# Loads cut by partitions: attention chunks in four transfers of 32, weight blocks in two of 64

## The chip, the cores and the metric

The kernel runs on one core of a Trainium2 chip. The time is that of one execution on the device in microseconds (us); a kernel's time is the median of its runs.

## The reference

The computation has two parts. The first is a linear attention (retention) with a decaying state per batch and head; the second is an MLP whose values are gated by a short convolution over time.

```python
gamma = 1.0 - 2.0 ** (-5.0 - np.arange(H))          # B, H, S, D = 4, 8, 768, 64
for t in range(S):
    state = gamma * state + einsum('bhd,bhe->bhde', k[:, :, t], v[:, :, t])
    y[:, :, t] = scale * einsum('bhd,bhde->bhe', q[:, :, t], state)
x = y.transpose(0, 2, 1, 3).reshape(B, S, H * D)     # 4 x 768 x 512
gate_pre = sum over k < 5 of conv_w[k] * xp[:, k:k + S, :]   # xp: x behind 4 rows of zeros
out = (sigmoid(gate_pre) * (x @ w_val)) @ w_out      # both weights 512 x 512
```

All inputs are float32; the two weight matrices and the convolution's weights reach the kernel as 64-bit words and are converted to float32 on the chip.

## The kernel before, in words

**Attention.** The sequence of each of the 4 batches is cut into 6 chunks of 128 tokens. Chunk number g (0 to 23) runs over the batches first: chunks 0 to 3 are the first 128 tokens of the four batches. `load(g)` (L163 to L168) brings a chunk's q, k by dimension, v and k by token into one tile `att` of 128 partitions with 8 KB each, 1,024 KB in all; chunk 0 comes in two halves of 4 KB rows. There are five such tiles (`LB`), so chunk g + 5 is loaded into the tile of chunk g when that is done with. Then GpSimd multiplies v by a decay (`decay`, L183), TensorE makes the scores (L193), VectorE masks them (`u`, L203), TensorE multiplies by v (L231), adds to the state `z_ps` (L215), ScalarE copies the state (`snap`, L226), TensorE reads it with q (L231), and VectorE moves the result into `x` (`evac`, L276). ScalarE and GpSimd split x into two parts for TensorE, `xh` (L287) and the remainder `xl` (L293).

**Weights.** `load_w(n)` (L300 to L306) brings one of eight blocks, 128 partitions with 4 KB each, 512 KB in all, into one of four `wst` tiles; blocks 0 to 3 are `w_val`, 4 to 7 `w_out`. Six steps, mostly on VectorE (L326, L332, L338, L342, the flush L355) with one on ScalarE (L347) and the sum on GpSimd (L351), make float32 values of it, then ScalarE and GpSimd split them (`wvh` or `woh` at L366, `wvl` or `wol` at L370).

**MLP.** It works in 6 units of 128 tokens of all batches, 4 tiles each. A tile has the convolution (`acc`, L381 on ScalarE and L383 on VectorE), the sigmoid (`gate`, L390, two buffers), the value product (L400, 12 matrix products), the gating (L414), the split of the gated values (`gvh` L417, `gvl` L421) and, a unit later, the output product (L431), a copy (L441) and the store (L445). The sigmoid of tile m reuses the gate buffer of tile m - 2, which GpSimd's L421 has read last. There are two x buffers.

**Order.** Each step is entered with a due time, an engine, a cost and the names that it reads and writes. `plan` makes one order of all steps from these, once, and each engine then works through its own steps strictly in that order. All transfers are issued by SyncE, in order too. A step that loads is one step in the plan, whatever `load` and `load_w` issue for it, so the plan doesn't know how a load is cut. The first loads stand in the plan as chunk 0, small tables, chunk 1, block 0, chunk 2, blocks 1 and 2, chunk 3, block 3, chunks 4 to 8, blocks 4 to 7, chunk 9, and from then on chunks and stores. At the start TensorE runs 13 matrix products without use (L451).

Of the kernel before, what the change touches and what calls it, by code (L numbers as in the profile page):

```python
# [10 lines left out]
I32 = mybir.dt.int32  # L11
# [4 lines left out]

P = 128
HALF = 64
NPAIR = 4
TAPS = 5  # L20
WARM = 13
# [3 lines left out]
TINY = 2.0 ** -15 * (1.0 + 1.0 / 8.0)  # L25
LO, HI = slice(0, HALF), slice(HALF, P)

# [51 lines left out]
def tile_retention_gated_mlp(  # L79
# [31 lines left out]
    nc = tc.nc  # L111
# [23 lines left out]
    pos_sb = const.tile([2, P + 512], F32, name="pos_sb")  # L135
    cw_sb = const.tile([P, NPAIR, TAPS], F32, name="cw_sb")
    base = const.tile([P, NPAIR, P], F32, name="base")
    wvh = const.tile([P, NPAIR, DM], F32R, name="wvh")
    wvl = const.tile([P, NPAIR, DM], F32R, name="wvl")
    woh = const.tile([P, NPAIR, DM], F32R, name="woh")  # L140
    wol = const.tile([P, NPAIR, DM], F32R, name="wol")

    z_ps = ps_s.tile([P, 2, B, 2, HALF], F32, name="z_ps")
    sy0 = ps_y.tile([P, 2, 512], F32, name="sy")
# [16 lines left out]
    tiles, us, snaps, xs, xh, xl, decs, pos_ps = {}, {}, {}, {}, {}, {}, {0: base}, []  # L161

    def load(g, part=slice(0, 4)):  # L163
        b, c = chunks[g]
        i = b * NCH + c
        if part.start == 0:
            tiles[g] = loads.tile([P, 4, 2, 2, P], F32, name="att")
        nc.sync.dma_start(out=tiles[g][:, part], in_=att[i, :, part])  # L168

    def get(dst, src):  # L170
        nc.sync.dma_start(out=dst, in_=src)
# [5 lines left out]
    def sy_of(g):  # L177
        return sy1 if g < EARLY and g % 2 else sy0

    def decay(g):  # L180
        b, c = chunks[g]
        v = tiles[g][:, 2].rearrange("p x j (s e) -> p (x j s) e", s=2)
        nc.gpsimd.tensor_tensor(  # L183
            v, v, vd_sb[:, c, :].unsqueeze(2).broadcast_to([P, 8, HALF]), op=ALU.mult
        )

    def scores(g):
        sy = sy_of(g)
        q, kT = halves(g, 0), halves(g, 1)
        for j in range(2):  # L190
            for s in range(2):
                for x, rows, cols in ((0, LO, LO), (1, HI, LO), (1, LO, HI), (0, HI, HI)):
                    nc.tensor.matmul(  # L193
                        sy[cols, x, (2 * j + s) * HALF:(2 * j + s + 1) * HALF],
                        lhsT=kT[rows, x, j, s, :],
# [4 lines left out]
    def mask(g):  # L200
        sy = sy_of(g)
        us[g] = mlp.tile([P, 2, 4, HALF], F32, name="u")
        nc.vector.tensor_tensor(  # L203
            us[g],
            sy[:, :, 0:256].rearrange("p x (a t) -> p x a t", t=HALF),
            tri_sb.unsqueeze(1).unsqueeze(1).broadcast_to([P, 2, 4, HALF]),
# [92 lines left out]

    def load_w(n):  # L300
        st = stage.tile([P, 512, 2], I32, name="wst", bufs=4)
        nc.sync.dma_start(
            out=st,
            in_=w64[n // 4, n % 4].bitcast(I32).rearrange("p (n two) -> p n two", two=2),
        )
        raws[n] = st  # L306

    cvt = {}
# [158 lines left out]
    def load_at(due, g):  # L467
        a = [("att", g % LB, "qk"), ("att", g % LB, "vk")]
        if g == 0:
            at(due, "DMA", 1.4, [], a[0:1], load, g, slice(0, 2))  # L470
            at(due, "DMA", 0.2, [], ["small"], get, small_sb, small)
            at(due, "DMA", 1.4, [], a[1:2], load, g, slice(2, 4))
            at(due, "DMA", 0.1, [], ["pos"], get, pos_sb, pos)
            at(due, "DMA", 0.1, [], ["cwraw"], get, cw_raw,
               conv_w.bitcast(I32).rearrange("p (n two) -> p n two", two=2))
        else:
            at(due, "DMA", 2.6, [], a, load, g)
# [63 lines left out]
    def load_w_at(t, n):  # L541
        at(t, "DMA", 1.3, [], [("wst", n % 4)], load_w, n)
# [60 lines left out]
    for p in range(4 * (NU - 1)):  # L603
        n, m = 1 + p // 4, p % 4
# [98 lines left out]
```

## Time and profile before

| | |
|---|---|
| Time, median of 3 runs | 237.65 us (237.08 to 238.66) |
| Profiled execution | 236.69 us, span 233.9 us |
| TensorE matmul busy | 209.4 us (90% of the span) |
| VectorE, GpSimd, ScalarE busy | 142.3, 105.9, 105.3 us |
| Read from HBM, written | 29.46 MB, 6.29 MB |
| Chunk, median from issue to landing | 5.4 us |
| Weight block, median from issue to landing | 8.7 us |

The page has the busy shares of the engines over 40 slices of the span, the traffic of the DMA engines, the chain of work that ended last, and groups of instructions. The trace behind it gives each engine's instructions in time, with the idle time before them and what ended it. Engine names in it are PE (TensorE's matrix products), PEld (its weight loads), DVE (VectorE), ACT (ScalarE), POOL (GpSimd) and SP (SyncE); a q behind a name is that engine's sequencer. TensorE's busy time counts pipelined products, so a busy TensorE isn't one at its peak.

### The profile page before, as it was taken

The page shows a single profiled execution, that of the slowest core. Times are in us where ns is not written, and L with a number is a line of the kernel's source. Part 1 is how long each engine was busy: PE and PEld are TensorE (multiplying, and loading weights), DVE is VectorE, ACT ScalarE, POOL GpSimd, SP SyncE. Part 2 cuts the span into 40 slices and gives each one's busy share as a digit, 9 for nine tenths or more (in the row PEclk, how much of TensorE's full clock was granted, in tenths as well). Part 3 has the DMA queues.
Part 4 walks back from the last instruction along what each step waited for, and adds up shares of the span by engine and source line. Part 5 has one row for each costly group of instructions (what it writes and reads, how often), then busy time and mean ns, then how long its engine had stood idle before and what let it go on. Part 6 is the DMA issues. An engine that isn't in the chain of part 4 may idle for free.

```text
span 233.9 us, 7910 instructions
## 1 busy us (share of the span) xinstructions
PE 209.4 (90%) x3547; PEld 163.2 (70%) x3547; DVE 142.3 (61%) x214; ACT 105.3 (45%) x210; POOL 105.9 (45%) x93
## 2 busy tenths in 40 slices
PE   8574779975955999999999999999999999999994
PEld 2363667754643877777777877877877778888884
DVE  0288879999699882699325895318991269811100
ACT  2333384554627362754346744237532456322222
POOL 0358986479929464543464254434413442222200
PEclk9778559997997999999999999999999999999999
DMA  5999968546540254653354346321011101111122
GB/s 159 387 418 415 402 251 331 181 134 230 186 179 1 84 205 168 227 224 129 115 216 182 95 177 228 132 101 48 0 48 48 47 1 61 63 58 45 45 90 90
DMA packets 8677, 36.24 MB, mean 155 GB/s; under 512 B 1090, under 2 KB 1474, under 8 KB 5700
## 3 DMA queue, kind: packets, MB, share of 16 engines
q1 hardware_dynamic: 8644, 35.75, 41.0%
q8 instruction: 27, 0.44, 0.8%
q14 instruction: 6, 0.05, 0.1%
HBM read 29.46 MB, written 6.29 MB: 153 GB/s over the span
## 4 chain that ended last, share of the span: by engine, by line
PE 79%; DVE 8%; DMA 5%; issue 4%; POOL 2%; SPq 1%; ACT 0%; ACTq 0%; DVEq 0%; POOLq 0%
PE mm L400 31%; PE mm L431 29%; PE sy L231 10%; PE z_ps L215 5%; DMA att<-in_att_dram 5%; PE sy L193 4%; DVE acc L383 1%; DVE u L203 1%; POOL rest L351 1%; DVE acc L338 1%; DVE rest L355 1%; DVE top L332 1%; DVE rest L342 1%; DVE x L276 1%; DVE acc L326 1%
## 5 line engine op out<-in xcount | busy, mean ns | idle before, releaser
L383 DVE SCALAR_TENSOR_TENSOR acc<-x,cw_sb,acc 128x512 f32<-128x512 f32 x96 | 71.0, 753 | 7.3 <-ACT acc L381 5.1
L421 POOL TENSOR_TENSOR gvl<-gate,gvh 128x512 fp32r<-128x512 f32 x24 | 31.0, 1292 | 43.1 <-ACT gvh L417 43.1
L293 POOL TENSOR_TENSOR xl<-x,xh 128x512 fp32r<-128x512 f32 x24 | 30.9, 1286 | 39.6 <-ACT xh L287 39.6
L431 PE MATMUL mm<-woh,gvh 128*128 128x512 f32 (+1 forms) x100 | 39.0, 390 | 4.9 <-ACT woh L366 4.9
L431 PE MATMUL mm<-wol,gvh 128*128 128x512 f32 (+1 forms) x100 | 39.0, 390 | 0.0
L431 PE MATMUL mm<-woh,gvl 128*128 128x512 f32 (+1 forms) x100 | 38.9, 389 | 0.0
L183 POOL TENSOR_TENSOR att<-att,small_sb 128x512 f32<-128x512 f32 x24 | 25.0, 1044 | 25.7 <-DMA att<-in_att_dram 24.4
L276 DVE TENSOR_TENSOR x<-sy,dec 128x512 f32<-128x512 f32 x20 | 13.7, 687 | 36.8 <-PE sy L193 29.3
L226 ACT COPY snap<-z_ps 128x256 f32<-128x256 f32 x44 | 16.1, 371 | 32.5 <-PE z_ps L215 32.5
L400 PE MATMUL mm<-xl,wvh 128*128 128x512 f32 x96 | 30.2, 411 | 0.0
L400 PE MATMUL mm<-xh,wvl 128*128 128x512 f32 x96 | 28.5, 413 | 0.0
L400 PE MATMUL mm<-xh,wvh 128*128 128x512 f32 x96 | 28.4, 420 | 0.1
L441 ACT COPY o_sb<-mm 128x512 f32<-128x512 f32 (+1 forms) x25 | 14.3, 571 | 27.3 <-PE mm L431 27.0
L414 DVE TENSOR_TENSOR gate<-mm,gate 128x512 f32<-128x512 f32 x24 | 16.5, 685 | 16.2 <-PE mm L400 16.1
L231 PEld LDWEIGHTS sy<-u,att 64*64 64x64 f32 x768 | 15.7, 153 | 13.6 <-issue 4.4
L431 PEld LDWEIGHTS mm<-woh,gvh 128*128 128x128 f32 x100 | 18.9, 189 | 8.9 <-ACT woh L366 5.3
L287 ACT CAST xh<-x 128x512 fp32r<-128x512 f32 x24 | 14.9, 620 | 21.9 <-DVE x L276 21.8
L215 PE MATMUL z_ps<-att 64*64 64x64 f32 x704 | 22.0, 242 | 2.6 <-issue 1.5
L231 PE MATMUL sy<-u,att 64*64 64x64 f32 x768 | 18.9, 244 | 6.1 <-DVE x L276 3.1
L215 PEld LDWEIGHTS z_ps<-att 64*64 64x64 f32 x704 | 17.0, 151 | 8.7 <-issue 5.0
L417 ACT CAST gvh<-gate 128x512 fp32r<-128x512 f32 x24 | 14.8, 618 | 18.2 <-DVE gate L414 18.2
L193 PE MATMUL sy<-att 64*64 64x64 f32 x768 | 17.9, 232 | 5.5 <-issue 2.8
(42 smaller groups left out, 264.7 us busy)
## 6 DMA issues: line engine op xcount, KB each, us to landing
att<-in_att_dram SPq DMA_DIRECT2D x23, 1024.0 KB, 5.4
out_dram<-o_sb SPq DMA_DIRECT2D x23, 256.0 KB, 2.0
wst<-in_w_dram SPq DMA_DIRECT2D x8, 512.0 KB, 8.7
att<-in_att_dram SPq DMA_DIRECT2D x2, 512.0 KB, 5.4
out_dram<-o_sb SPq DMA_DIRECT2D x2, 128.0 KB, 1.7
small_sb<-in_small_dram SPq DMA_DIRECT2D x1, 68.0 KB, 4.1
cw_raw<-in_conv_w_dram SPq DMA_DIRECT2D x1, 20.0 KB, 5.9
pos_sb<-in_pos_dram SPq DMA_DIRECT2D x1, 5.0 KB
```

Of the source, the lines that this page charges most:

```text
L183: nc.gpsimd.tensor_tensor(v, v, vd_sb[:, c, :].unsqueeze(2).broadcast_to([P, 8, HALF]), op=ALU.mult)
L193: nc.tensor.matmul(sy[cols, x, (2 * j + s) * HALF:(2 * j + s + 1) * HALF], lhsT=kT[rows, x, j, s, :], rhs=q[rows, x, j, s, :], start=True, ...
L215: nc.tensor.matmul(z_ps[cols, x, b, j], lhsT=k[rows, x, j, s, :], rhs=v[rows, x, j, s, :], start=g == 0 and s == 0 and j == 0, stop=True, ...
L226: nc.scalar.copy(sn, z_ps[:, :, b])
L231: nc.tensor.matmul(sy_of(g)[cols, h, off:off + HALF], lhsT=lhsT, rhs=rhs, start=start, stop=True, skip_group_check=True,)
L276: nc.vector.tensor_tensor(xs[c][:, :, b, HALO:].rearrange("p (h j) t -> p h j t", h=2), sy_of(g)[:, :, 256:512].rearrange("p h (j t) -> p ...
L293: nc.gpsimd.tensor_tensor(xl[c][:, :, b], xs[c][:, :, b, HALO:], xh[c][:, :, b].bitcast(F32), op=ALU.subtract)
L383: nc.vector.scalar_tensor_tensor(acc, x[:, :, k:k + P], cw_sb[:, m, k:k + 1], acc, op0=ALU.mult, op1=ALU.add,)
L400: nc.tensor.matmul(vps[n, m], lhsT=w[:, m, ct * P:(ct + 1) * P], rhs=xx[n][:, ct].rearrange("p b t -> p (b t)"), start=(i == 0), stop=(i = ...
L414: nc.vector.tensor_tensor(gv, vps.pop((n, m)), gv, op=ALU.mult)
L421: nc.gpsimd.tensor_tensor(gvl[:, m, :], gate.pop((n, m)), gvh[:, m, :].bitcast(F32), op=ALU.subtract)
L431: nc.tensor.matmul(ops[n, b, cs.start][:, 0:cs.stop - cs.start], lhsT=gg[:, ct, b * P:(b + 1) * P], rhs=w[:, ct, cs], start=(i == 0), stop ...
```

## The change

Each load of a chunk is issued as four transfers of 32 partitions (256 KB each; for the two halves of chunk 0, 128 KB each), each load of a weight block as two transfers of 64 partitions (256 KB each). Rows, bytes, tiles, buffers and the plan's table of steps are the same; all transfers go through SyncE's queue as before. In the changed kernel the lines behind the edits have numbers higher by one or two: the chunks' transfers are issued at L170, the blocks' at L306, the decay is L185.

```diff
+ROWS = 32
...
     def load(g, part=slice(0, 4)):
...
-        nc.sync.dma_start(out=tiles[g][:, part], in_=att[i, :, part])
+        for p in range(0, P, ROWS):
+            nc.sync.dma_start(out=tiles[g][p:p + ROWS, part], in_=att[i, p:p + ROWS, part])
...
     def load_w(n):
         st = stage.tile([P, 512, 2], I32, name="wst", bufs=4)
-        nc.sync.dma_start(
-            out=st,
-            in_=w64[n // 4, n % 4].bitcast(I32).rearrange("p (n two) -> p n two", two=2),
-        )
+        src = w64[n // 4, n % 4].bitcast(I32).rearrange("p (n two) -> p n two", two=2)
+        for p in range(0, P, 2 * ROWS):
+            nc.sync.dma_start(out=st[p:p + 2 * ROWS], in_=src[p:p + 2 * ROWS])
         raws[n] = st
```

## The prediction

> **What bounds the kernel now.** I read the page first: the busy shares over time, then what the DMA engines moved, then the chain that ended last.
>
> ```profile
> PE   8574779975955999999999999999999999999994
> DVE  0288879999699882699325895318991269811100
> POOL 0358986479929464543464254434413442222200
> DMA  5999968546540254653354346321011101111122
> GB/s 159 387 418 415 402 251 331 181 134 230 186 179 1 84 205 168 227 224 129 115 216 182 95 177 228 132 101 48 0 48 48 47 1 61 63 58 45 45 90 90
> PE 79%; DVE 8%; DMA 5%; issue 4%; POOL 2%; SPq 1%; ACT 0%; ACTq 0%; DVEq 0%; POOLq 0%
> ```
>
> Each slice is 5.85 us. From slice 13 (76 us) TensorE is full to the end, so work that reaches that phase later ends the kernel later by as much. Before it no engine is full throughout; VectorE comes nearest. The loads fill the DMA engines in slices 1 to 4, near 400 GB/s, and leave room in most slices after that. So if the change touches the loads, it acts in the first 75 us.
>
> The chain in order of time shows how the loads set that phase, and the waits show who stands there.
>
> ```profile
> 3.81 10.75 DMA att<-in_att_dram
> 14.62 1.04 POOL att L183
> 15.71 1.29 POOL rest L351
> 17.03 0.69 DVE rest L355
> POOL att L183 <- DMA att<-in_att_dram: 24.4, 15, 7.8
> ```
>
> The third chunk is issued at 3.81 and lands at 14.56; GpSimd's decay of it is released by the landing, and the weights' sum (L351) and VectorE's flush (L355) follow. GpSimd waits for chunks 15 times, 24.4 us in all. It runs in a written order: a late chunk holds up everything behind that chunk's decay, also work that doesn't need the chunk. That is where I expect a slower load to bite.
>
> **The change part by part.** No byte, matrix product or elementwise instruction is added, removed or moved; what changes is the shape of the loads and the waits on them.
>
> *Issues and waits.* SyncE issues 25 chunk transfers and 8 weight transfers now, 100 and 16 afterwards.
>
> ```profile
> att<-in_att_dram SPq DMA_DIRECT2D x23, 1024.0 KB, 5.4
> wst<-in_w_dram SPq DMA_DIRECT2D x8, 512.0 KB, 8.7
> L168 SPq DMA_DIRECT2D att<-in_att_dram x25: 327/328/752, 0.7 to 148.5; - x25
> L193 PEldq EVENT_SEMAPHORE  x5: 51/51/51, 10.8 to 59.4; - x5
> L183 POOLq EVENT_SEMAPHORE  x20: 17/17/43, 8.2 to 154.3; - x20
> ```
>
> An issue takes 0.33 us at the median, so four take 1.3 us where one took 0.33. A 256 KB piece at the 421 GB/s that are quoted below flows in 0.62 us, longer than its issue: issuing is hidden under the flow. The order also shows that every transfer waits for the one eight before it; eight are now 2 MB in flight, 5 us of flow at 421 GB/s, against the 2.9 us that a chunk takes beyond its own flow (median 5.4 us to landing, 2.5 of them flow). So the queue stays filled, and I cost this at nothing. Each reader of a chunk waits for four landings instead of one. Scores gain two separate waits of 51 ns per chunk: at most 24 x 2 x 0.051 = 2.4 us if TensorE always stands for them; at least nothing, where it still has matrix work queued. GpSimd's 17 ns waits, about three more per chunk, are 1.2 us over the whole run on an engine at 45%. I take 0.5 us for all waits in the case where nothing else happens; in the forecast they lie inside longer stalls and count nothing.
>
> *The rate of the loads* is the term that decides. No row shows a transfer onto part of the partitions, apart from 5 KB of positions. These rows are the nearest:
>
> ```profile
> 2.00:4.00 2.00, 2.00 (x6) 0.76 (x5) 0.00 (x0) 0.22 (x2) 0.00 (x0) 1.00 0.86 229
> 4.00:6.00 2.00, 1.72 (x6) 0.50 (x4) 0.00 (x0) 0.00 (x0) 0.00 (x0) 1.00 0.86 245
> 10.00:20.00 10.00, 5.98 (x237) 5.44 (x241) 7.81 (x13) 3.71 (x9) 5.88 (x5) 0.75 1.02 421
> ```
>
> The last two columns are the DMA engines' busy share and GB/s. With whole chunks and blocks in the queue the engines move 421 GB/s. In the first 4 us, with chunk 0's halves and small tables one behind the other, they are busy 86% and move only 229 to 245: busy engines can run at little more than half of the rate. From above, the bound is the 421. From below: if each of the 128 partitions accepts no more than it does today, a piece on 32 is held to a quarter, 105 GB/s. If all DMA engines work on a piece, as they do on a chunk, they write to the same 32 partitions together and afterwards to the next 32, so I expect crowding, though not down to a quarter: nothing shows that partitions, rather than engines, are at their limit now. I take the row of short transfers, 229.
>
> [...]
>
> *From the rate to the end.* On SyncE's queue, in the place where chunk 8, the second four weight blocks and chunk 9 are loaded, before:
>
> ```order
> L168 DMA att<-in_att_dram 128x2048 [waits DMAHW0_49,DMAHW2_49,PE_49,Pool_49]
> L302 DMA wst<-in_w_dram 128x1024 [waits DMAHW1_49,Activation_49]
> L302 DMA wst<-in_w_dram 128x1024 [waits Activation_49]
> L302 DMA wst<-in_w_dram 128x1024 [waits DMAHW3_49,Activation_49]
> L302 DMA wst<-in_w_dram 128x1024 [waits DMAHW4_49,Activation_49]
> L168 DMA att<-in_att_dram 128x2048 [waits DMAHW5_49,PE_49,Pool_49]
> ```
>
> And changed, from the second of those weight blocks to chunk 9:
>
> ```order
> L306 DMA wst<-in_w_dram 64x1024 [waits DMAHW5_49,Activation_49]
> L306 DMA wst<-in_w_dram 64x1024 [waits DMAHW6_49]
> L306 DMA wst<-in_w_dram 64x1024 [waits DMAHW7_49,Activation_49]
> L306 DMA wst<-in_w_dram 64x1024 [waits DMAHW0_49]
> L306 DMA wst<-in_w_dram 64x1024 [waits DMAHW1_49,Activation_49]
> L306 DMA wst<-in_w_dram 64x1024 [waits DMAHW2_49]
> L170 DMA att<-in_att_dram 32x2048 [waits DMAHW3_49,PE_49,Pool_49]
> ```
>
> DMAHW0 to 7 are the eight landing semaphores, used in turn; the order of transfers is the same, and chunk 9 still comes behind chunks 1 to 8 and all eight weight blocks. On GpSimd the order is the same too; here are the decays of chunks 7, 8 and 9 (the last row) with the first remainder of gated values (gvl) between them, before and changed:
>
> ```order
> L370 TENSOR_TENSOR wvl<-rest,wvh 128x512 [waits Activation_49] x2
> L183 TENSOR_TENSOR att<-att,small_sb 128x512 [waits DMAHW7_49,PE_49]
> L183 TENSOR_TENSOR att<-att,small_sb 128x512 [waits DMAHW0_49,PE_49]
> L421 TENSOR_TENSOR gvl<-gate,gvh 128x512 [waits Activation_49]
> L183 TENSOR_TENSOR att<-att,small_sb 128x512 [waits DMAHW5_49,PE_49]
> ```
>
> ```order
> L371 TENSOR_TENSOR wvl<-rest,wvh 128x512 [waits Activation_49] x2
> L185 TENSOR_TENSOR att<-att,small_sb 128x512 [waits DMAHW5_49,DMAHW4_49,DMAHW6_49,DMAHW3_49,PE_49]
> L185 TENSOR_TENSOR att<-att,small_sb 128x512 [waits DMAHW2_49,DMAHW1_49,DMAHW7_49,DMAHW0_49,PE_49]
> L422 TENSOR_TENSOR gvl<-gate,gvh 128x512 [waits Activation_49]
> L185 TENSOR_TENSOR att<-att,small_sb 128x512 [waits DMAHW5_49,DMAHW4_49,DMAHW6_49,DMAHW3_49,PE_49]
> ```
>
> Each decay waits for four landings now, and nothing else has moved. The issue of chunk 9, the decays of chunks 0 and 9, and what stands behind the latter on GpSimd, ScalarE, VectorE and TensorE (start, duration, in brackets the idle time before it):
>
> ```profile
> 40.67 8.84 SPq L168 DMA_DIRECT2D att<-in_att_dram  x2
> 8.27 1.04 POOL L183 TENSOR_TENSOR att<-att,small_sb 128x512 f32<-128x512 f32 x1 [7.83 <-DMA att<-in_att_dram]
> 45.66 1.04 POOL L183 TENSOR_TENSOR att<-att,small_sb 128x512 f32<-128x512 f32 x1 [1.99 <-DMA att<-in_att_dram]
> 46.66 1.29 POOL L421 TENSOR_TENSOR gvl<-gate,gvh 128x512 fp32r<-128x512 f32 x1
> 54.12 1.28 POOL L351 TENSOR_TENSOR rest<-rest,top 128x512 f32<-128x512 f32 x1
> 48.95 0.60 ACT L390 ACTIVATE gate<-acc 128x512 f32<-128x512 f32 x1
> 50.83 0.68 DVE L414 TENSOR_TENSOR gate<-mm,gate 128x512 f32<-128x512 f32 x1
> 55.40 0.68 DVE L276 TENSOR_TENSOR x<-sy,dec 128x512 f32<-128x512 f32 x1
> 59.87 0.69 DVE L276 TENSOR_TENSOR x<-sy,dec 128x512 f32<-128x512 f32 x1 [1.87 <-PE sy L231]
> 72.64 0.49 PE L431 MATMUL mm<-woh,gvh 128*128 128x512 f32 x1 [4.85 <-ACT woh L366]
> ```
>
> Chunk 0 is decayed at 8.27 in either kernel, since its stretch already runs at 229 to 245. Behind it, up to chunk 9, come nine chunks of 1.049 MB and eight blocks of 0.524 MB. At 229 GB/s a chunk takes 4.58 us and a block 2.29, together 41.2 + 18.3 = 59.5, so chunk 9 is decayed at 67.8 and not at 45.66: 22.1 later. Its buffer doesn't set this: it is free for the issue at 40.67 now, and would have to come free over 20 us later. Behind the decay L421 ends at 68.8 + 1.3 = 70.1. The fourth sigmoid reuses the gate buffer that L421 has read (two buffers), 70.1 to 70.7, then VectorE's L414 starts at 70.7, where it stood at 50.83: 19.9 later. The other 2.2 us were slack between L421, sigmoid and L414. From there VectorE works almost without a gap to 72 us, through the conversions of the output weights; its one larger gap (1.87 us at 59.87) is a round trip to TensorE that itself began with L276 at 55.40, so it moves along, and the sum L351 at 54.12 moves by 20.9 on GpSimd. TensorE's stand of 4.85 us ends with weights from that same work. Nothing takes the delay back before TensorE is full.
>
> Later loads are hidden even at that rate:
>
> ```profile
> 99.52 0.33 SPq L168 DMA_DIRECT2D att<-in_att_dram  x1
> 104.96 1.04 POOL L183 TENSOR_TENSOR att<-att,small_sb 128x512 f32<-128x512 f32 x1 [0.59 <-DMA att<-in_att_dram]
> 110.01 1.29 POOL L421 TENSOR_TENSOR gvl<-gate,gvh 128x512 fp32r<-128x512 f32 x1 [4.00 <-ACT gvh L417]
> ```
>
> A chunk issued at 99.52 would be decayed at 108.1 in place of 104.96 (1.0 us of later issue, 4.58 for 2.49 us of flow), to 109.1, and GpSimd's next work starts at 110.01.
>
> The sum: 19.9 us. On the profiled execution (236.69 us, span 233.9) that makes 256.6; that run lies 0.4% under the median of 237.65 (237.08 to 238.66), and on the median it makes **257.5 us**.
>
> **The rivals.** The rate at which the delay begins follows from the same rows: chunk 9 may be 2.2 us late, so 13.6 MB must flow in 39.6 us, 344 GB/s.
>
> [...]
>
> (2) Partial overlap. With eight pieces queued, engines drift apart, and the rate is midway between 229 and 421, 325 GB/s: chunk 3.23, block 1.61, chunk 9 at 50.2, 4.6 late, less 2.2: +2.4, 240.0 us.
>
> (3) The pieces cost nothing: the rate stays above 344, only waits are left, 238.2 us. For it: a piece still runs on all engines, and the bytes per row are the same, 8 KB. Against: nothing quoted shows partial transfers at speed.
>
> (4) Faster: the 229 to 245 GB/s at the start come from large transfers behind each other, and pieces lift them to 421. Chunk 0 with its tables (1.14 MB) then takes 2.7 us and not 4.9; the chain from the third chunk starts 2.2 us earlier, 235.4 us. It decides only if the rate afterwards stays above 344 too; the same engines then run at 421 with large transfers, which speaks against it.
>
> **How the numbers follow.** Forecast 0.46, half rate 0.25, partial overlap 0.12, nothing 0.14, faster 0.03. The range 240 to 266 us holds the forecast and the first two rivals, 0.83; its top is a rate of about 200 GB/s. The quarter rate is left out. A measurement here can tell about 1% (2.4 us) from no change: faster 0.03, same 0.14, slower 0.83.
>
> **What would show it.** Right: GB/s near 230 in slices 2 to 11 in place of 400 and less, at the same high DMA share; the decay of chunk 9 near 68 us with a long wait for its transfer; total waits of L185 for chunks well over 24.4 us; TensorE full from about 96 us; the stretch from there to the end as long as before. Wrong: GB/s above 344 in slices 2 to 4, or chunk 9 decayed before 48 us. If chunk 9 is as late as said but TensorE is full much earlier than 96 us, my account of VectorE's order is the step that failed. If the last phase grows, the waits on TensorE weigh more than I say.

## The result and the profile after

The change makes the kernel slower: 260.39 us median (259.44 to 262.22, 4 runs) against 237.37 (236.88 to 238.66, 4 runs), ratio 1.097 with a 95% interval of 1.0894 to 1.1046. The forecast was 257.5 us (240 to 266), so slower by somewhat more than said. The profiled execution took 262.22 us, with a span of 260.3; it is the slowest of the four, and set against the one before (span 233.9) it shows +26.4 us where the medians differ by 23.0. Some runs of the kernels below took over 1.5% longer than the fastest of the same kernel; they are left out of the ratios, of the kernel with two transfers of 64 neighbours only one run (257.45 us) and no ratio remains, and the profiles of that kernel, of every fourth partition and of the alternating halves are of such runs.

First the page of the changed kernel: busy shares, DMA share and traffic over 40 slices of 6.5 us, and the shares of the chain that ended last.

```profile
PE   7573551999327929999999999999999999999995
DMA  7999999999937760786755875658001111111132
GB/s 171 219 220 230 220 209 218 219 215 243 220 71 165 174 151 3 168 227 152 190 147 137 204 165 141 170 141 204 22 21 43 43 43 40 43 40 40 40 118 86
PE 64%; DMA 25%; DVE 3%; SPq 2%; issue 2%; POOL 1%; ACT 1%; POOLq 0%; ACTq 0%; DVEq 0%
```

Slices 1 to 10 (6.5 to 71 us) are a plateau at 209 to 243 GB/s with the DMA engines busy 90% or more (digit 9); before, the loads ran near 400 and were done with their bulk in slice 6. DMA has gone from 5% of the chain to 25%. The stretches of time say the same (window, its length, busy time and count of PE, PEld, DVE, ACT and POOL, then granted TensorE clock, DMA share, GB/s):

```profile
10.00:20.00 10.00, 5.90 (x186) 5.28 (x178) 4.75 (x7) 3.32 (x9) 1.04 (x1) 0.61 1.02 214
30.00:40.00 10.00, 5.37 (x151) 4.72 (x152) 5.06 (x8) 2.13 (x4) 5.42 (x5) 0.50 1.05 222
60.00:70.00 10.00, 6.81 (x190) 4.97 (x188) 5.37 (x8) 2.23 (x5) 0.00 (x0) 0.95 1.05 234
```

A DMA share of 1.02 stands beside 214 GB/s here, and stood beside 421 before: the share tells that the engines hold packets, not how fast bytes move. In 60 to 70 us GpSimd does nothing at all. The chain in order of time shows why:

```profile
12.76 10.71 DMA wst<-in_w_dram
...
61.77 9.49 DMA att<-in_att_dram
71.42 1.04 POOL att L185
72.46 1.23 POOL gvl L422
```

Six transfers follow each other without a gap from 12.76 to 71.26, each 9 to 11 us from issue to landing, since eight transfers are in the queue at a time; the last is chunk 9's, and its decay is next. GpSimd's waits for chunks, and the instructions that the prediction followed (start, duration, idle time before):

```profile
POOL att L185 <- DMA att<-in_att_dram: 68.6, 20, 11.6
```

```profile
71.42 1.04 POOL L185 TENSOR_TENSOR att<-att,small_sb 128x512 f32<-128x512 f32 x1 [11.60 <-DMA att<-in_att_dram]
72.42 1.26 POOL L422 TENSOR_TENSOR gvl<-gate,gvh 128x512 fp32r<-128x512 f32 x1
74.34 0.69 DVE L415 TENSOR_TENSOR gate<-mm,gate 128x512 f32<-128x512 f32 x1 [7.35 <-ACT gate L391]
97.24 0.79 PE L432 MATMUL mm<-woh,gvh 128*128 128x512 f32 x1 [4.75 <-ACT woh L367]
```

Chunk 9's decay moved from 45.66 to 71.42 (+25.8), the gating from 50.83 to 74.34 (+23.5), the first output product with `woh` from 72.64 to 97.24 (+24.6). From there to the end of the span it takes 163.1 us, against 161.3 before (+1.8). 24.6 and 1.8 are the 26.4. The chain that ended last goes on from the sigmoid (73.72) through ScalarE and not through the gating: ScalarE stood 8.59 us for L422, the copy of the state stands behind that sigmoid in its order, and TensorE stands 8.21 us for the copy, up to 76.18.

### The profile page after: what moved, and what is told of

The parts are those of the page before. It is cut to its first block, busy times and chain, and to the rows that moved or that the text cites. A ratio compares the mean times of both kernels' runs of the same rounds, so it can differ in the third digit from the quotient of the medians.

```text
span 260.3 us, 8078 instructions
## 1 busy us (share of the span) xinstructions
PE 218.5 (84%) x3547; PEld 170.0 (65%) x3547; DVE 142.8 (55%) x214; ACT 105.3 (40%) x210; POOL 105.9 (41%) x93
## 3 DMA queue, kind: packets, MB, share of 16 engines
q1 hardware_dynamic: 9972, 35.76, 57.8%
## 4 chain that ended last, share of the span: by engine, by line
PE 64%; DMA 25%; DVE 3%; SPq 2%; issue 2%; POOL 1%; ACT 1%; POOLq 0%; ACTq 0%; DVEq 0%
PE mm L432 26%; PE mm L401 23%; DMA att<-in_att_dram 13%; DMA wst<-in_w_dram 11%; PE sy L233 8%; PE z_ps L217 4%; PE sy L195 3%; SPq L170 2%; DVE acc L384 1%; DVE acc L327 1%; DVE x L278 1%; DVE rest L356 1%; POOL rest L352 0%; POOL gvl L422 0%; SPq L173 0%
## 5 line engine op out<-in xcount | busy, mean ns | idle before, releaser
L185 POOL TENSOR_TENSOR att<-att,small_sb 128x512 f32<-128x512 f32 x24 | 25.0, 1044 | 76.6 <-DMA att<-in_att_dram 68.6
L422 POOL TENSOR_TENSOR gvl<-gate,gvh 128x512 fp32r<-128x512 f32 x24 | 31.0, 1293 | 34.8 <-ACT gvh L418 34.8
L432 PE MATMUL mm<-woh,gvh 128*128 128x512 f32 (+1 forms) x100 | 39.6, 396 | 4.7 <-ACT woh L367 4.7
L432 PE MATMUL mm<-wol,gvh 128*128 128x512 f32 (+1 forms) x100 | 39.6, 396 | 0.0
L217 PE MATMUL z_ps<-att 64*64 64x64 f32 x704 | 23.4, 250 | 13.5 <-ACT snap L228 8.7
L217 PEld LDWEIGHTS z_ps<-att 64*64 64x64 f32 x704 | 18.4, 159 | 19.6 <-ACT snap L228 10.2
L195 PE MATMUL sy<-att 64*64 64x64 f32 x768 | 21.5, 247 | 9.6 <-DMA att<-in_att_dram 6.8
L401 PE MATMUL mm<-xh,wvl 128*128 128x512 f32 x96 | 29.3, 423 | 0.0
L195 PEld LDWEIGHTS sy<-att 64*64 64x64 f32 x768 | 18.2, 157 | 13.1 <-issue 11.8
L233 PEld LDWEIGHTS sy<-u,att 64*64 64x64 f32 x768 | 16.5, 159 | 15.3 <-issue 4.0
L233 PE MATMUL sy<-u,att 64*64 64x64 f32 x768 | 19.8, 251 | 7.7 <-DVE u L205 2.9
L289 ACT CAST xh<-x 128x512 fp32r<-128x512 f32 x24 | 14.9, 619 | 19.9 <-DVE x L278 19.9
```

The costliest lines, as they stand in the source:

```text
L185: nc.gpsimd.tensor_tensor(v, v, vd_sb[:, c, :].unsqueeze(2).broadcast_to([P, 8, HALF]), op=ALU.mult)
L195: nc.tensor.matmul(sy[cols, x, (2 * j + s) * HALF:(2 * j + s + 1) * HALF], lhsT=kT[rows, x, j, s, :], rhs=q[rows, x, j, s, :], start=True, ...
L217: nc.tensor.matmul(z_ps[cols, x, b, j], lhsT=k[rows, x, j, s, :], rhs=v[rows, x, j, s, :], start=g == 0 and s == 0 and j == 0, stop=True, ...
L233: nc.tensor.matmul(sy_of(g)[cols, h, off:off + HALF], lhsT=lhsT, rhs=rhs, start=start, stop=True, skip_group_check=True,)
L401: nc.tensor.matmul(vps[n, m], lhsT=w[:, m, ct * P:(ct + 1) * P], rhs=xx[n][:, ct].rearrange("p b t -> p (b t)"), start=(i == 0), stop=(i = ...
L422: nc.gpsimd.tensor_tensor(gvl[:, m, :], gate.pop((n, m)), gvh[:, m, :].bitcast(F32), op=ALU.subtract)
```

## The experiments

**The theories.** *Reach*: what sets the rate is which of the 128 partitions a transfer touches; onto 32 or 64 neighbours it flows at about half, whatever its size (214 to 234 GB/s in the stretches above, 421 with whole loads). It is a theory: the trace gives rates and packet times, and not what holds a packet up. The "ways" and "paths" of the expectations below are my picture for it, and no row shows them. *Count and size*: more and smaller transfers in the queue are slower whatever they touch, because fewer bytes are in flight or each piece has a fixed cost. *Waits*: the readers' additional waits cost the time. Beside these stands the question whether the written order, chunk 9's decay ahead of L422, turns late bytes into late work.

### Cut along the row instead of by partitions

```diff
-        nc.sync.dma_start(out=tiles[g][:, part], in_=att[i, :, part])
+        for x in range(part.start, part.stop):
+            nc.sync.dma_start(out=tiles[g][:, x], in_=att[i, :, x])
...
+        for h in (slice(0, 256), slice(256, 512)):
+            nc.sync.dma_start(out=st[:, h], in_=src[:, h])
```

> Four transfers per chunk and two per block as in the change, 256 KB each, but cut along the row: each goes to all 128 partitions, with 2 KB rows. Two theories of the slow loads. Reach: a transfer onto a part of the partitions can be written at half the rate only, whatever its size; here every transfer spans all partitions, so the loads run at 380 to 420 GB/s between 10 and 30 us, chunk 9 is decayed before 48 us, and the time is 236 to 239 us. Count: it is the number of transfers, their 256 KB or the 2 MB in flight that slow the loads; then they stay at 210 to 230 GB/s and the time is 257 to 262 us. The finer pieces also let the decay of a chunk wait for its v alone, which can only help.

Measured 238.19 us (235.27 to 239.25) against 237.5, ratio 1.0003 (0.9955 to 1.0052). The stretches:

```profile
10.00:20.00 10.00, 6.13 (x224) 5.49 (x224) 7.70 (x13) 3.13 (x8) 5.67 (x5) 0.77 1.04 384
20.00:30.00 10.00, 6.52 (x224) 5.60 (x224) 8.69 (x15) 4.40 (x9) 8.19 (x9) 0.74 1.04 367
```

Nearly as many transfers as in the change, each of the same 256 KB, and the rate stays at 367 to 384 GB/s: a little under the 380 to 420 expected, above the 344 that the prediction had as its threshold. Chunk 9 is decayed at 45.58. Count and size fall as the cause. The waits are tested less fully here: a chunk lands in four pieces, but its decay waits for one to four of them, where in the change it waits for all four.

### Chunks alone, in 32 and in 64 neighbours

```diff
+        for p in range(0, P, ROWS):
+            nc.sync.dma_start(out=tiles[g][p:p + ROWS, part], in_=att[i, p:p + ROWS, part])
```

> Only the chunks are cut in four by 32 partitions, the weight blocks stay whole. With 4.87 us for a cut chunk (its landings in the changed kernel lie that far apart) and 1.25 us for a whole block at 421 GB/s, chunk 9 is decayed at 7.8 + 43.8 + 10.0 = 61.6 us, VectorE's fourth gating follows 2.9 us later at 64.5, where it stood at 50.8 before: 13.7 us later, with 1 to 2 us from later waits 251 to 253 us. If a chunk and a block don't simply add up along the queue, the time lies elsewhere: near 260 if the chunks alone set it.

The second kernel has `p` in steps of 64. Weight blocks are whole in both.

> Chunks cut in two by 64 partitions, weight blocks whole. If what counts is how many of the write ways a transfer reaches, and 64 neighbouring partitions reach no more than 32 do, the time equals that of the kernel with chunks cut by 32 and whole blocks, 251 to 253 us, with loads near 215 GB/s while chunks alone flow. If crowding goes with the number of partitions, 64 are crowded half as much: a chunk takes about 3.7 us, chunk 9 is decayed near 51 us, and the time is 239 to 242 us. By count, half as many transfers of twice the size also give the middle.

Measured 258.63 us (256.73 to 262.23), ratio 1.0885 (1.0795 to 1.0975), and 264.29 us (257.45 to 265.93); 237.5 us before. The stretch in which only chunks are loaded, 32 first, then 64:

```profile
30.00:40.00 10.00, 4.86 (x134) 4.02 (x127) 5.75 (x9) 2.13 (x4) 4.96 (x5) 0.50 1.03 216
40.00:50.00 10.00, 7.96 (x88) 6.31 (x88) 5.18 (x8) 5.58 (x13) 8.12 (x7) 0.64 1.03 220
```

```profile
30.00:40.00 10.00, 5.49 (x154) 4.93 (x155) 5.38 (x9) 2.13 (x4) 5.76 (x5) 0.50 1.02 216
40.00:50.00 10.00, 5.81 (x79) 4.87 (x79) 5.30 (x8) 5.59 (x13) 7.83 (x7) 0.57 1.02 221
```

Twice as many partitions, and twice the bytes, in each transfer buy nothing: 216 and 221 against 216 and 220. That fits the reach theory if 64 neighbours are held as far down as 32, as they are in these rows. Both times are longer than the 251 to 253 expected, though, in all eight runs; the sum that I had made for chunks alone is wrong (below).

### Every fourth and every second partition

```diff
-        for p in range(0, P, ROWS):
-            nc.sync.dma_start(out=tiles[g][p:p + ROWS, part], in_=att[i, p:p + ROWS, part])
+        for p in range(4):
+            nc.sync.dma_start(out=tiles[g][p::4, part], in_=att[i, p::4, part])
```

> Chunks cut in four transfers of 32 partitions again, but each takes every fourth partition of all 128; weight blocks whole. If crowding is by neighbouring partitions (reach), each transfer now spreads over the whole memory and the rate comes back for the most part, 330 to 421 GB/s: 237 to 241 us. If it is the number of partitions in one transfer, or their count and size, nothing changes against chunks cut by 32 neighbours: 251 to 253 us.

The second kernel has `range(2)` and `p::2`.

> Chunks in two transfers of 64 partitions, every second one (0, 2, 4, ... and 1, 3, 5, ...), weight blocks whole: same count and size as the kernel with two transfers of 64 neighbouring partitions (264.3 us, chunk 9 decayed at 68.0). If it counts which partitions a transfer reaches: above 340 GB/s from 10 to 40 us, chunk 9 decayed at 45 to 53, 237 to 241 us. If it counts how many partitions or how many bytes it has: 257 to 265 us, chunk 9 at 65 to 68.

Measured 241.09 us (239.29 to 244.16) against 237.5, ratio 1.0147 (1.0068 to 1.0226), and 237.25 us (235.37 to 238.57) against 237.43, ratio 1.0005 (0.996 to 1.0049). The stretches, fourth first, then second:

```profile
10.00:20.00 10.00, 5.86 (x205) 5.18 (x205) 4.90 (x9) 3.31 (x8) 2.35 (x3) 0.61 0.94 340
20.00:30.00 10.00, 6.35 (x236) 5.75 (x239) 8.99 (x15) 4.01 (x9) 9.26 (x8) 0.73 1.03 417
```

```profile
10.00:20.00 10.00, 5.90 (x224) 5.33 (x224) 6.79 (x11) 2.59 (x6) 5.39 (x5) 0.72 1.01 408
20.00:30.00 10.00, 5.79 (x207) 5.24 (x208) 8.35 (x14) 3.63 (x7) 7.94 (x8) 0.62 1.01 398
```

This is the cleanest pair: the same count, the same 64 partitions and 512 KB in each transfer as in the slow kernel above, other partitions, and 398 to 408 GB/s instead of 216. Which partitions a transfer touches decides here. One thing goes along with it: a transfer that leaves out partitions also leaves out the source's rows, and no run parts the two. The length of the source alone is not it, though: a whole block is 512 KB in one piece of the source, and its 4 KB packets take 160 ns (before, median from 16 to 30 us); 64 neighbours of a chunk are 512 KB in one piece as well, and their 8 KB packets take 619, twice as long per byte.

With every fourth partition the decays wait for up to four landings, as in the change, so such waits cost no more than this kernel loses. Its loss of 1.5% fits another source, the issue. Two rows of SyncE's issues (form, duration in ns as least, median and most, first and last start), of every fourth and of 32 neighbours:

```profile
L170 SPq DMA_DIRECT2D att<-in_att_dram x100: 468/592/1537, 0.7 to 159.2; - x100
```

```profile
L170 SPq DMA_DIRECT2D att<-in_att_dram x100: 310/413/1949, 0.7 to 169.6; - x100
```

(The second row is of the kernel that follows.) An issue of a strided piece takes 0.59 us at the median, and a 256 KB piece flows in 0.62 us at 421 GB/s. With the halves of chunk 0, 128 KB each, issuing is the slower of the two: this kernel moves 184 GB/s at a DMA share of 0.62 from 4 to 6 us, its chunk 1 is issued from 7.23 to 9.61 us where that was done at 2.86 before, and its decay of chunk 9 comes at 52.33.

In the stretches shown, the six kernels with cut chunks up to here fall into two groups: 214 to 234 GB/s where the pieces are of neighbouring partitions, 340 to 417 where each piece reaches over all 128.

### The order of the pieces

```diff
-        for p in range(0, P, ROWS):
+        for p in (0, 64, 32, 96):
```

> Chunks in four transfers of 32 neighbouring partitions, issued in the order 0, 64, 32, 96 instead of 0, 32, 64, 96; weight blocks whole. Same count and size as the kernel with chunks alone cut (258.6 us, chunk 9 decayed at 66.05). If pieces in the queue overlap and each meets another part of the partitions' paths, consecutive pieces on different halves run side by side: the rate climbs toward 330 to 420 GB/s, chunk 9 is decayed at 46 to 54, 238 to 247 us. If every DMA engine works through its queue one packet after another, the order of the pieces changes nothing: 257 to 260 us, chunk 9 at 65 to 68.

Blocks are whole, as in the kernel with chunks alone cut. Measured 253.22 us (251.04 to 254.94) against 237.43, ratio 1.0625 (1.0549 to 1.0702): between the two expectations.

```profile
30.00:40.00 10.00, 4.87 (x135) 4.20 (x137) 5.75 (x9) 2.13 (x4) 4.76 (x5) 0.50 1.02 244
40.00:50.00 10.00, 8.49 (x89) 6.94 (x88) 7.15 (x11) 6.87 (x15) 10.00 (x9) 0.60 1.03 243
```

244 instead of 216: with pieces of the two halves in turn the loads flow 13% faster, and 5.4 of 21.1 us come back. The trace's records of single packets bear on this. This is the median time of an 8,192-byte packet that started between 16 and 30 us:

```
                                   ns
before                            313
the change                        620
chunks alone, 32 neighbours       619
chunks alone, 64 neighbours       619
alternating halves                562
every fourth / every second       309 / 313
```

In the three kernels with pieces of neighbours in order a packet takes twice as long as before, at the same size (619 to 620 ns against 313), and with the halves alternating it takes 9% less than that (562). What holds a packet up, and why the order shortens it by 9%, no row shows.

### Blocks alone, and late chunks alone

The first leaves the chunks whole and loads the blocks in two transfers of 64. The second:

```diff
+        rows = P if g < 10 else ROWS
+        for p in range(0, P, rows):
+            nc.sync.dma_start(out=tiles[g][p:p + rows, part], in_=att[i, p:p + rows, part])
```

> Only the weight blocks are cut, in two by 64 partitions; chunks stay whole. If a cut block takes 2.35 us and a whole chunk 2.49, chunk 9 is decayed at 8.0 + 22.4 + 18.8 = 49.2 us, the fourth gating 2.9 us later at 52.1 where it stood at 50.8: 238 to 239.5 us. If mixing whole and cut transfers leaves some DMA engines behind the others, as it did by 3 to 4 us when whole blocks stood between cut chunks, chunk 9 comes 2 to 4 us later still: 241 to 243 us.

> Chunks 10 to 23 are cut in four by 32 partitions, chunks 0 to 9 and all weight blocks stay whole. If only the crowded first 75 us turn the slow rate into time, as predicted, the loads of these chunks are hidden and only the readers' extra waits are left: 237.5 to 239.5 us, with TensorE full from about 73 us as before. If slow loads cost something wherever they stand, 14 of 24 chunks carry more than half of the loss: 248 us or more.

Blocks alone: 244.5 us (244.18 to 244.81) against 236.57, ratio 1.0329 (1.0312 to 1.0346), above both expectations. Late chunks alone: 239.29 us (237.87 to 240.38), ratio 1.0105 (1.0061 to 1.0149). The decay of chunk 9, with blocks alone and with chunks alone:

```profile
54.34 1.04 POOL L184 TENSOR_TENSOR att<-att,small_sb 128x512 f32<-128x512 f32 x1 [4.58 <-DMA att<-in_att_dram]
```

```profile
66.05 1.04 POOL L185 TENSOR_TENSOR att<-att,small_sb 128x512 f32<-128x512 f32 x1 [8.19 <-DMA att<-in_att_dram]
```

I had expected 49.2 and 61.6, by adding slow and fast transfers one behind the other. Both come about 5 us later. Alone, chunks cost 21.1 us and blocks 7.9 us, together 23.0 and not 29. One thing differs with chunks alone: a transfer counts as landed with the last of its 16 completions, and these get out of step. Of one chunk piece most lie between 23.88 and 24.35 and the last at 26.89; of the pieces and blocks that land between 21 us and chunk 9 they lie 1.9 to 5.6 us apart, in the full change 1.6 to 2.1. But this doesn't explain both kernels. With blocks alone they lie 1.4 to 2.9 us apart in the same stretch, against 0.5 to 1.8 before, and with every second partition they lie up to 3.25 us apart at no loss. With blocks alone a part is that the queue doesn't stay full, which my sum had not: the DMA share is 0.66 from 36 to 40 us. What makes up the 5 us in either kernel stays open.

Late chunks alone leave TensorE's restart where it was (72.65) and lose 2.5 us behind it, within the first expectation. The trace of TensorE there, and below it a stand of the kernel before:

```profile
72.65 0.79 PE L434 MATMUL mm<-woh,gvh 128*128 128x512 f32 x1 [4.85 <-ACT woh L369]
...
92.64 0.55 PE L196 MATMUL sy<-att 64*64 64x64 f32 x22
95.25 0.39 PE L196 MATMUL sy<-att 64*64 64x64 f32 x10 [2.06 <-issue]
```

```profile
23.71 0.37 PE L193 MATMUL sy<-att 64*64 64x64 f32 x2 [2.14 <-issue]
```

TensorE stands 2.06 us in the middle of a chunk's scores; "issue" says that the profile found no releaser. It is not a late chunk: the four pieces of this one had landed by 86.16, and the product at 95.25 waits for no semaphore. The trace's packets name another candidate. The page has a DMA queue called "instruction", with 28 packets of 16 KB in this kernel; one of them starts at 92.57 and takes 1.38 us. In the twelve profiles here there are 39 stands of over 0.3 us at which TensorE waits for no semaphore. All end 2.3 to 3.0 us after the start of such a packet, and they recur at the same places in TensorE's program, some 127 matrix products apart (at 219 to 221 products, 346 to 348, 472 to 475 and so on). So I read them as TensorE waiting for its own next instructions. The page counts their packets on the same 16 DMA engines as the loads (0.8% of the engines' span before and in the change, where the loads' and stores' queue has 41.0% and 57.8%). In the kernel before, the packet for this place starts at 87.67, in time for it; here it starts 4.9 us later, while cut chunks are on their way. That they hold it up fits, but was not tried by itself.

So late chunks cost little, and not by the readers' waits: TensorE waits for no chunk behind its restart. With 14 of 24 chunks cut only 2.5 us are lost; most of the 23 arises before TensorE is full.

### The written order

The decays of chunks 9 and on are placed behind the previous chunk's `evac` in the plan, in the changed kernel and in the one before:

```diff
-        at(t - 3.0, "POOL", 1.05, ["small"], [vk], decay, g)
+        b0, c0 = chunks[g - 1]
+        held = [("x", c0, b0)] if g >= 9 else []
+        at(t - 3.0, "POOL", 1.05, ["small"] + held, [vk], decay, g)
```

> All loads cut as in the change, but GpSimd's decay of chunk 9 and later ones is placed in the order behind the attention result of the chunk before it, so that chunk 9's landing no longer stands ahead of the gated values' remainders. If the stand of 11.6 us for chunk 9 in the written order is what the last part of the loss comes from, the fourth gating follows the earlier chunks alone, some 16 us later than before and not 23.5: 253 to 256 us. If the loads themselves are the bound, or work behind chunk 9 needs it anyway, it stays at 259 to 262 us.

> The same later place of the decays with whole loads: what the reordering is worth by itself, so that the kernel with cut loads and late decays is read rightly. GpSimd's stands for chunks were 24.4 us in all but mostly cost nothing, 2.0 us of them ahead of the second remainder of gated values: 235 to 238.5 us.

With the cut loads 256.36 us (255.42 to 256.8) against 236.57, ratio 1.082 (1.0788 to 1.0851); with whole loads 237.07 (235.74 to 238.36), ratio 1.0025 (0.9997 to 1.0053). GpSimd and VectorE of the first:

```profile
POOL att L185 <- DMA att<-in_att_dram: 31.6, 8, 7.2
```

```profile
65.44 0.68 DVE L415 TENSOR_TENSOR gate<-mm,gate 128x512 f32<-128x512 f32 x1
90.27 0.50 PE L432 MATMUL mm<-woh,gvh 128*128 128x512 f32 x1 [4.81 <-ACT woh L367]
```

The time is just above the first expectation. GpSimd waits 37 us less for chunks, the gating starts 8.9 us earlier than in the change, TensorE's restart comes 7.0 earlier, and the median is 4.0 lower. So the place of chunk 9's decay is a real step, but it carries only a part: without it TensorE's restart is still 17.6 us later than before. By the order, what is left are chunks 1 to 8 and the blocks, which land as late as before this edit. The chain that ended last shows something more:

```profile
33.41 9.45 DMA att<-in_att_dram
...
67.44 2.59 issue
```

It follows loads without a break up to 42.86 us only. Behind them it is mostly computing, and in it TensorE stands for 2.59 us without a wait, again behind a packet of instructions (67.32). I didn't take these parts further apart.

No version here is faster than the kernel before: the cut along the row, every second partition, and the late decays with whole loads take the same time, within their intervals.

## Why the prediction was right, and which term was off

**What bounds it.** Right: most of the loss arises before TensorE is full, as the kernel with late chunks alone shows, and TensorE's full phase begins later by about as much as the end moves (24.6 of 26.4).

**Issues and waits.** Right: 100 issues of 0.41 us at the median (0.33 in the prediction) hide under the flow, at a DMA share of 1.01 to 1.05 in each ten microseconds from 10 to 70. With late chunks alone TensorE waits for no chunk in its full phase, and with every fourth partition all waits together stay within 1.5%. The 0.5 us of rival 3 is too small to be told from nothing here.

**The rate.** This term was mis-sized, and its reason was weak. I took 229 GB/s from the first 6 us of the kernel before. That row came from chunk 0's halves on all 128 partitions with small tables between them; it says nothing of partial transfers, and lies near the measured rate by chance. In this term the forecast came close by luck. The 13.63 MB between chunk 0's decay (7.80) and chunk 9's landing (71.26) took 63.5 us where the sum had 59.5, so 215 GB/s. The delay is 25.8 us instead of 22.1. That loads onto neighbouring partitions flow slower was right; the crowding by which the prediction explains it was its estimate, and no run shows it as the cause. Half rate, which had a chance of 0.25, came nearer than my 229: no row from before the result shows it, but in the change a packet takes 620 ns where it took 313, and the rate is 215 GB/s, where half of the 421 of whole loads would be 210.5. Partial overlap, midway at 325 because engines drift apart, is not what came: even with halves alternating the rate is 244. On the profiled executions the sum of 19.9 us stands against 26.4: 3.6 of the difference arise up to the gating, by the rate, 1.1 up to TensorE's restart and 1.8 behind it. On the medians it stands against 23.0.

**From the rate to the end.** The places were right up to the sigmoid: L422 behind chunk 9's decay, then the sigmoid and the gating, with 2.3 us of slack (25.8 against 23.5; 2.2 said). From there the chain ran through ScalarE and its copy of the state, where the prediction followed VectorE; both hang on the same sigmoid. "Nothing takes the delay back" held: 1.1 us are added up to TensorE's restart, at 97.24 where the sum had about 96. What the prediction did not see is that chunk 9 is only the last of several late steps: with its decay out of the way, 4 us of 23 come back.

**As long as before.** The last stretch grew by 1.8 us, against the prediction. TensorE stands once more for 0.41 us, at 112.98 and without a wait, 2.8 us after a packet of instructions began (110.17). No wait for a chunk was added there, so "the waits on TensorE", which the prediction named for this case, are not it. By an estimate from the rows below the granted clock gives most of the rest. Two-microsecond windows from the restart on, before and changed:

```profile
72.64:74.64 2.00, 1.95 (x5) 1.34 (x5) 2.00 (x4) 1.88 (x4) 2.00 (x2) 0.61 0.00 0
74.64:76.64 2.00, 2.00 (x51) 1.39 (x49) 1.93 (x4) 0.92 (x2) 2.00 (x3) 0.54 0.03 8
76.64:78.64 2.00, 2.00 (x38) 1.46 (x38) 1.93 (x3) 0.37 (x1) 1.77 (x2) 1.00 0.00 0
```

```profile
97.24:99.24 2.00, 2.00 (x5) 1.44 (x5) 1.09 (x2) 1.60 (x3) 1.96 (x2) 0.50 0.00 0
99.24:101.24 2.00, 2.00 (x50) 1.37 (x48) 1.61 (x3) 0.92 (x2) 2.00 (x3) 0.50 0.03 8
101.24:103.24 2.00, 2.00 (x10) 1.59 (x6) 1.93 (x4) 0.59 (x2) 2.00 (x3) 0.54 0.00 0
```

The clock (the third number from the end) is low for 6 us instead of 4: 2 x (0.11 + 0.04 + 0.46) = 1.2 us of work at full clock, as TensorE is busy in all six rows. With 0.41 that is 1.6 of 1.8. Why the clock came back later was not tried.

**Later loads.** Hidden, as said: TensorE waits for no chunk behind its restart, neither in the change nor with late chunks alone. What the prediction left out are the packets of TensorE's instructions: with late chunks alone one starts at 92.57 instead of 87.67, and TensorE stands for 2.06 us behind it. That the slow loads delay it was not tried by itself.

## What to carry to other kernels

Where loads bound a stage, cut a transfer along its row, or by every second partition, and leave each transfer spread over all 128 partitions: cutting it into neighbours halved the rate here whether the pieces had 32 or 64 partitions (216 GB/s with either, against 367 to 408 along the row and by every second). Read GB/s and not the DMA share, which was full in both cases (1.02 at 214 GB/s and at 421). To find what a late transfer costs, follow the work written behind its first reader, and then ask what is late next, since taking the first such step away gave back a sixth of the loss. Where TensorE stands without a wait, look at the packets of the instruction queue before blaming a load: here all 39 such stands ended 2.3 to 3.0 us after one began.

## What the runs showed of the hardware that I had not expected

- 64 neighbouring partitions load no faster than 32 (216 and 216 GB/s), while 64 taken as every second reach 398 to 408.
- An issue takes longer for strided partitions: 0.57 to 0.59 us at the median against 0.41 to 0.47 for pieces of neighbours and 0.33 for a whole chunk. While chunk 0's pieces of 128 KB were issued so, the rate was 184 to 199 GB/s at a DMA share of 0.62 to 0.65.
- Alternating the halves in one queue brings 13% of rate (216 to 244 GB/s).
- A transfer lands with the last of its 16 completions, and with chunks alone cut these lay up to 5.6 us apart, in the full change up to 2.1. The costs of the two kinds of cut do not add up (21.1 and 7.9 alone, 23.0 together).
- TensorE's stands without a wait, up to 4.37 us long in the change (at 43.70), all end 2.3 to 3.0 us after a 16 KB packet of the instruction queue began.
